# Moving 1 MB of output weights to the end of a decode kernel's load stream, laying W2 out anew, and turning the second MLP layer round

## The chip, the cores and the metric

The kernel runs on one core of a Trainium2 chip. The metric is the device time of one execution in microseconds (us); single executions of the kernel before spread over 1 to 1.5 us, so most experiments were timed in five rounds beside the kernel before on the same chip. The profile is one execution. Its time axis starts at the span's start, and all moments below ("at 664.7") are microseconds on that axis. The record calls an execution slow when it is over 1.5% above the fastest of its kernel.

## The reference, cut to what matters

```python
mod = silu(c) @ w_mod                      # six vectors per batch row: sa, ca, ga, sb, cb, gb
h = layernorm(x) * (1 + ca) + sa
x = x + ga * attention(h, k_cache, v_cache, wq, wo)   # 8 batch rows, 32 heads, 8 KV heads, 8192 cached keys
h = layernorm(x) * (1 + cb) + sb
r = relu(h @ w1 + b1)                      # 512 -> 1792
x = x + gb * ((r * r) @ w2 + b2)           # 1792 -> 512
```

Everything is bf16. The caches are 268 MB and are read once; the rest is small. The change aims at the last 30 us: the end of attention (`wo`), the first MLP layer (`w1`), the second (`w2`).

## The kernel before

One queue (SP's) loads nearly everything in order: modulation and query weights, then K and V tiles of 4 MB through a ring of four slots, and at the very end W1 and W2. The last V tile is loaded in four pieces. The 4096 x 512 output weights `wo` are loaded near the start, the last 1 MB of them separately.

```python
load(0); load(1)
...
d_woe = dma("sync", s_woe, ... A_wo[0:24 * DH, :] ...)            # 3 MB
d_wo = dma("sync", s_wo, lambda e: e.dma_start(                   # last 1 MB, packets of 1 KB
    wo_sb[:, 24:32, :], A_wo[24 * DH:, :].rearrange("(h dh) n -> dh h n", dh=DH)))
load(2); load(3)
...                                                               # at the last V tile:
d_w1 = dma("sync", s_w1, lambda e: e.dma_start(W1v, B_w1.rearrange("(k p) f -> p k f", p=128)), ...)
w2_r = B_w2.rearrange("(k p j) n -> p k j n", p=128, j=2)
d_w2 = [dma("sync", s_w2[i], lambda e, a=a, z=z: e.dma_start(W2v[:, a:z], w2_r[:, a:z]))
        for i, (a, z) in enumerate(((0, 4), (4, 7)))]             # 1 MB, then 0.75 MB
```

The MLP has the hidden units on partitions and the 8 batch rows as columns, in both layers. There are FT = 14 groups f of 128 hidden units. W2 comes in runs of two rows (2 KB), so a partition p of group f holds hidden unit 256*(f//2) + 2*p + f%2, and the first layer must read W1's columns with a step of 2 elements:

```python
for hh in range(2):
    for f in range(7 * hh, 7 * (hh + 1)):
        wcol = lambda k, f=f: W1v[:, k, 256 * (f // 2):256 * (f // 2 + 1)].rearrange(
            "p (q j) -> p j q", j=2)[:, f % 2, :]
        for k in range(KT):                                       # KT = 4
            t = op("tensor", lambda e: e.matmul(hT_ps[hh][:, f % 7, :], wcol(k), hbT[:, k, :], ...), [k_hb, d_w1])
    ... relu and square of the half, on VectorE ...
for f in range(FT):
    for k in range(KT):                                           # W2 is the stationary side, 8 columns stream
        t = op("tensor", lambda e: e.matmul(yT_ps[:, k, :], W2v[:, f // 2, f % 2, k * 128:(k + 1) * 128],
               hidT[:, f, :], ...), [k_sq[f // 7], d_w2[0 if f < 8 else 1]])
y2T = yT_ps * mod(5); yoT = y2T + x1T                             # 128 x 32, two VectorE operations
... four transposes, one copy on ACT, one on VectorE, two output DMAs of 4 KB
```

In a matmul call the stationary operand stands first (after the output), the streamed one second.

## Time and profile before

| | kernel before |
|---|---|
| median of 3 runs | 672.09 us (671.75 to 672.13) |
| span of the profiled execution | 669.4 us |
| share of the 16 DMA engines used by SP's queue | 99.0% |
| end of the chain | last W2 chunk lands, then about 2.1 us to the issue of the output |

The profile page's line of SP's DMA queue (packets, MB, share of 16 engines' span):

```profile
q1 hardware_dynamic: 13236, 283.65, 99.0%
```

The queue is full from start to end. Its stream decides the time; what counts beyond it is what must follow its last bytes. The end of the chain of waits, in order of time (start, duration, what):

```profile
642.46 1.41 SPq L552
643.92 21.47 DMA ring<-in_B_w_dram
665.43 0.82 PE PS L654 x24
```

The chain runs through the issue of the W2 DMAs, their landing, and the matmuls that waited for it. The timeline of the last microseconds (start, duration, engine, line, operation, output<-inputs, count, and in brackets how long the engine had idled and what ended that; PE is the matmul, PEld, further below, the load of a stationary operand):

```profile
661.91 1.68 PE L646 MATMUL PS<-hbT,ring 128*128 128x8 bf16 x56
...
663.61 0.99 PE L654 MATMUL PS<-hidT,ring 128*128 128x8 bf16 x32
...
665.43 0.81 PE L654 MATMUL PS<-hidT,ring 128*128 128x8 bf16 x24 [0.83 <-DMA ring<-in_B_w_dram]
666.28 0.19 DVE L658 TENSOR_TENSOR y2T<-PS,modT 128x32 f32<-128x32 f32 x1 [2.18 <-PE PS L654]
...
666.75 0.38 PE L665 MATMUL PS<-IDENT,yoT 128*8 128x128 bf16 x4 [0.51 <-DVE yoT L659]
667.16 0.37 ACT L672 ACTIVATE out_sb<-PS 8x256 bf16<-8x256 bf16 x1 [6.25 <-PE PS L665]
...
667.51 0.33 SPq L673 DMA_DIRECT2D out_dram<-out_sb  x1
```

L646 is the first layer: 56 matmuls in 1.68 us. L654 is the second: its first 32 matmuls run when the hidden values are there (663.6), its last 24 wait for the second W2 chunk until 665.43. Two small VectorE operations, transposes, copies, and the output is issued at 667.51.

The stages of the end (window, then its length and the busy time of PE, PEld, DVE, ACT and POOL with instruction counts, the granted TensorE clock with 1.00 as full speed, the share of the DMA engines in use, GB/s):

```profile
661.00:663.00 2.00, 2.00 (x50) 2.00 (x48) 0.66 (x4) 0.00 (x0) 0.00 (x0) 0.50 0.72 268
663.00:665.40 2.40, 1.59 (x55) 1.44 (x51) 0.76 (x4) 0.00 (x0) 0.00 (x0) 0.50 0.24 86
665.40:668.80 3.40, 1.19 (x28) 0.82 (x28) 0.66 (x3) 0.37 (x1) 0.00 (x0) 0.50 0.01 2
```

The clock is at half, and the DMA share falls to 0.72 and 0.24 while the stream still runs: the 16 engines don't finish together. The trace records 16 reports for each of these DMAs; those for the last W2 chunk come between 661.71 and 665.39. The waiting matmuls start after the last of them.

Two groups of 32 value matmuls of the same kernel, one at the low clock, one at the high one:

```profile
638.40 3.60 PE L525 MATMUL PS<-ring,Pm 128*32 128x512 bf16 x32 [0.54 <-DVE rinv L506]
...
642.98 1.91 PE L525 MATMUL PS<-ring,Pm 128*32 128x512 bf16 x32
```

They stream 512 columns each, in four column groups side by side: 3.60 us against 1.91.

### The profile page before, as it was taken

To read this page: it belongs to the slowest core of one execution; us is meant where nothing else is said; L and a number is where in the kernel's file an instruction comes from. 1 tells how busy PE (TensorE), PEld (TensorE's weight loads), DVE (VectorE), ACT (ScalarE), POOL (GpSimd) and SP (SyncE) were. 2 spreads that over 40 slices of the span, in tenths; PEclk is the share of its full clock that TensorE was granted. 3 is DMA by queue.
4 is the path that set the end of the run, shared out by engine and by line. 5 is a ranking of instruction groups with operands and counts; after the bars stand their busy time and mean duration, and the time that the engine had idled before them with its cause. 6 is when DMAs were issued, how large, how long until landed. Compare 5 with 4: busy or idle time off the path is not lost.

```text
span 669.4 us, 15944 instructions
## 1 busy us (share of the span) xinstructions
PE 480.1 (72%) x7372; PEld 344.2 (51%) x7372; DVE 299.3 (45%) x566; ACT 234.9 (35%) x280; POOL 16.7 (2%) x66
## 2 busy tenths in 40 slices
PE   2394963798639963699448987499736995389877
PEld 2383731675318741477316762287415773177545
DVE  2162731467316661367315672166513673146722
ACT  2061620366106640266204660056402662046610
POOL 7200000000000000000000000000000000000000
PEclk9996966799759986799867995599775997679986
DMA  9999999999999999999999999999999999999996
GB/s 375 433 402 436 419 434 432 433 427 435 431 435 431 425 433 437 433 429 431 433 435 433 423 435 431 437 427 429 433 437 435 423 431 433 437 433 425 431 416 245
DMA packets 13305, 283.95 MB, mean 424 GB/s; under 512 B 1218, under 2 KB 2275, under 8 KB 4708
## 3 DMA queue, kind: packets, MB, share of 16 engines
q1 hardware_dynamic: 13236, 283.65, 99.0%
q8 instruction: 13, 0.21, 0.1%
q14 instruction: 8, 0.07, 0.0%
q10 hardware_dynamic: 48, 0.02, 0.0%
HBM read 283.66 MB, written 0.01 MB: 424 GB/s over the span
## 4 chain that ended last, share of the span: by engine, by line
PE 55%; DMA 38%; DVE 3%; ACT 2%; issue 1%; SPq 0%
PE PS L427 36%; DMA ring<-in_A_k_cache_dram 35%; PE PS L442 9%; PE PS L486 4%; PE PS L525 4%; DMA ring<-in_B_w_dram 3%; ACT KTb L432 1%; ACT P_sb L477 1%; DVE m L447 1%; PE PS L505 1%; DVE Pm L499 0%; DVE rinv L506 0%; DVE rhs_r L503 0%; DVE Dm L470 0%; PE PS L472 0%
## 5 line engine op out<-in xcount | busy, mean ns | idle before, releaser
L432 ACT ACTIVATE KTb<-PS 128x1024 bf16<-128x1024 bf16 x192 | 196.5, 1024 | 372.4 <-PE PS L427 372.4
L427 PE MATMUL PS<-IDENT,ring 128*128 128x128 bf16 x4096 | 267.9, 228 | 51.6 <-DMA ring<-in_A_k_cache_dram 51.6
L427 PEld LDWEIGHTS PS<-IDENT,ring 128*128 128x128 bf16 x4096 | 247.3, 102 | 99.9 <-DMA ring<-in_A_k_cache_dram 52.7
L434 DVE COPY KTb<-PS 128x1024 bf16<-128x1024 bf16 x320 | 210.1, 687 | 152.0 <-PE PS L427 149.8
L525 PE MATMUL PS<-ring,Pm 128*32 128x512 bf16 x992 | 87.1, 513 | 58.5 <-DMA ring<-in_A_v_cache_dram 54.1
L534 DVE CAST O_sb<-PS 128x512 bf16<-128x512 f32 x31 | 21.4, 692 | 138.1 <-PE PS L525 138.1
L442 PE MATMUL PS<-KTb,Qb 128*32 128x512 bf16 x1024 | 78.8, 384 | 4.5 <-ACT KTb L432 4.5
L525 PEld LDWEIGHTS PS<-ring,Pm 128*32 128x32 bf16 x992 | 30.4, 120 | 96.3 <-DMA ring<-in_A_v_cache_dram 55.4
L486 PE MATMUL PS<-IDENT,P_sb 128*64 128x128 bf16 x512 | 26.2, 278 | 10.3 <-ACT P_sb L477 10.0
L538 PEld LDWEIGHTS PS<-SEL,O_sb 128*128 128x128 bf16 x124 | 5.3, 99 | 46.2 <-DVE O_sb L534 46.2
L486 PEld LDWEIGHTS PS<-IDENT,P_sb 128*64 128x64 bf16 x512 | 22.3, 147 | 13.0 <-ACT P_sb L477 13.0
L477 ACT ACTIVATE P_sb<-PS,negm 128x512 bf16<-128x512 f32 x32 | 21.5, 685 | 18.9 <-DVE negm L474 18.9
L499 DVE COPY Pm<-PS 64x512 bf16<-64x512 bf16 x48 | 20.2, 421 | 16.9 <-PE PS L486 15.9
L442 PEld LDWEIGHTS PS<-KTb,Qb 128*32 128x32 bf16 x1024 | 15.4, 94 | 21.1 <-ACT KTb L432 8.5
L538 PE MATMUL PS<-SEL,O_sb 128*128 128x8 bf16 x124 | 8.0, 170 | 24.9 <-DVE O_sb L534 24.9
L447 DVE TENSOR_REDUCE m<-PS 128x1 f32<-128x512 f32 x32 | 22.0, 689 | 6.6 <-PE PS L442 6.6
L496 ACT ACTIVATE Pm<-PS 64x512 bf16<-64x512 bf16 x16 | 9.5, 592 | 6.5 <-PE PS L486 6.4
L541 DVE TENSOR_TENSOR oTn<-PS,rinv 128x8 bf16<-128x8 f32 x31 | 6.0, 194 | 11.0 <-PE PS L538 11.0
L505 PE MATMUL PS<-rhs_r,ONES 128*128 128x32 f32 x16 | 4.6, 380 | 6.8 <-DVE rhs_r L503 6.8
L387 PE MATMUL PS<-haT,ring 128*128 128x8 bf16 x128 | 3.6, 168 | 7.5 <-DMA ring<-in_A_wq_dram 7.5
L472 PE MATMUL PS<-Dm,R 128*128 128x4 bf16 x8 | 1.4, 178 | 10.1 <-DVE Dm L470 10.1
L634 ACT ACTIVATE std<-PS,epst 128x8 f32<-128x8 f32 x1 | 0.3, 267 | 22.4 <-PE PS L632 22.4
(111 smaller groups left out, 97.1 us busy)
## 6 DMA issues: line engine op xcount, KB each, us to landing
ring<-in_A_k_cache_dram SPq DMA_DIRECT2D x32, 4096.0 KB, 34.1
ring<-in_A_v_cache_dram SPq DMA_DIRECT2D x31, 4096.0 KB, 28.1
ring<-in_A_wq_dram SPq DMA_DIRECT2D x1, 4096.0 KB, 20.3
ring<-in_w_mod_dram SPq DMA_DIRECT2D x1, 3072.0 KB, 10.4
wo_sb<-in_A_wo_dram SPq DMA_DIRECT2D x1, 3072.0 KB, 45.1
ring<-in_A_v_cache_dram SPq DMA_DIRECT2D x1, 2048.0 KB, 22.4
ring<-in_B_w_dram SPq DMA_DIRECT2D x1, 1792.0 KB, 18.9
wo_sb<-in_A_wo_dram SPq DMA_DIRECT2D x1, 1024.0 KB, 47.7
```

Source lines behind the costliest of these rows:

```text
L427: t = op("tensor", lambda e, j=j, i=i: e.matmul(STG[j][:, i, :], src[:, 32 * k + 8 * j + i, :], IDENT[:, :], is_transpose=True), [loaded[n ...
L432: stg_free[j] = op("scalar", lambda e, j=j, dst=dst: e.activation(dst, STG[j], ACT.Copy), [t], "scaP")
L434: stg_free[j] = op("vector", lambda e, j=j, dst=dst: e.tensor_copy(dst, STG[j]), [t], "vecP")
L442: t = op("tensor", lambda e, hf=hf, q=q, rhs=rhs: e.matmul(PS[32 * q:32 * (q + 1), k, :], Qb[:, 2 * p + hf, :], rhs, start=(p == 0 and hf ...
L447: return op("vector", lambda e: e.tensor_reduce(m4[:, k:k + 1], bank(k), AX.X, ALU.max), [t])
L477: exps.append(op("scalar", lambda e, k=k: e.activation(P_sb[:, k, :], bank(k), ACT.Exp, bias=negm[:, 0:1], scale=inv_sqrt, accum_out=rs4[: ...
L486: t = op("tensor", lambda e, k=k, i=i, hf=hf, src=src: e.matmul(STG[k][64 * hf:64 * (hf + 1), i, :], src, IDENT[:, :], is_transpose=True, ...
L499: done.append(op("vector", lambda e, dst=dst, frm=frm: e.tensor_copy(dst, frm), [t, k_pm], "vecP"))
L505: t = op("tensor", lambda e: e.matmul(tot_ps, ONES[:, :], rhs_r[:]), [t])
L525: t = op("tensor", lambda e, p=p, m=m, cg=cg, vt=vt, Obank=Obank: e.matmul(Obank[32 * cg:32 * (cg + 1), :], lhs[:, p, 32 * m:32 * m + 32], ...
L534: t = op("vector", lambda e, osb=osb, Obank=Obank: e.tensor_copy(osb, Obank), [t], "vecP")
L538: t = op("tensor", lambda e, i=i, osb=osb, oT_ps=oT_ps: e.matmul(oT_ps, osb[:, i * 128:(i + 1) * 128], SEL[:, i, :], start=(i == 0), stop= ...
```

## The change

Its intent: (1) the last values arrive earlier if the last 1 MB of `wo` comes behind them; (2) W2 in one run of 14 rows per partition needs fewer, larger DMA packets; (3) with the batch rows on partitions the second layer streams W2 instead of loading it, and its result needs no transposes; (4) a small last W2 chunk (2 of 14 groups) leaves little to do after the last landing.

```diff
-        d_wo = dma("sync", s_wo, ... last 1 MB of A_wo ...)        # was ahead of load(2)
...
+                    d_wo = dma("sync", s_wo, ... last 1 MB of A_wo ...)   # now ahead of d_w1
                     d_w1 = dma("sync", s_w1, ...)
-                    w2_r = B_w2.rearrange("(k p j) n -> p k j n", p=128, j=2)
+                    w2_r = B_w2.rearrange("(p f) n -> p f n", p=128)
...
-                            for i, (a, z) in enumerate(((0, 4), (4, 7)))]
+                            for i, (a, z) in enumerate(((0, F2), (F2, FT)))]      # F2 = FT - 2
...
-                wcol = lambda k, f=f: W1v[:, k, 256 * (f // 2):256 * (f // 2 + 1)].rearrange(
-                    "p (q j) -> p j q", j=2)[:, f % 2, :]
+                wcol = lambda k, f=f: W1v[:, k, :].rearrange("p (q f) -> p f q", f=FT)[:, f, :]
...
         for f in range(FT):
-            for k in range(KT):
-                    yT_ps[:, k, :], W2v[:, f // 2, f % 2, k * 128:(k + 1) * 128], hidT[:, f, :],
-                    [k_sq[f // 7], d_w2[0 if f < 8 else 1]])
-        ... y2T, yoT on 128 x 32, four transposes, two copies ...
+            for cc in range(2):
+                    yN_ps[64 * cc:64 * cc + B, :], hidT[:, f, :], W2v[:, f, 256 * cc:256 * (cc + 1)],
+                    ... tile_position=(0, 64 * cc) ..., [k_sq[f // 7], d_w2[0 if f < F2 else 1]])
+        t = y2N = yN_ps * gbN          # 72 x 256
+        t = out_sb = y2N + x1N         # 72 x 256
```

With it go: b1's 14 small loads at the same step as W1's columns; `gb` computed with batches on partitions at the start; the transposes of x, moved up between the layer norm's steps; 4 filler matmuls instead of 6 there (fillers multiply the identity by itself, nobody reads the result; they are there to keep PE busy).

Partition p now holds W2's rows 14*p to 14*p+13, so group f is the hidden units 14*p + f.

More of the change, by code (lines that the diff above doesn't have):

```diff
@@ L210, in bass_adaLN_cond__gqa_block_cached__dense_activation_squared_relu__decode_kernel @@
         xT = sb("xT", [128, KT, B], BF16)
-        modT = sb("modT", [128, 24, B], FP32)
+        modT = sb("modT", [128, 20, B], FP32)
+        gbN = sb("gbN", [128, 256], FP32)
         ca1 = sb("ca1", [128, KT, B], FP32)
@@ L227, in bass_adaLN_cond__gqa_block_cached__dense_activation_squared_relu__decode_kernel @@
         hbT = sb("hbT", [128, KT, B], BF16)
-        rT = sb("rT", [128, FT, B], FP32)
         hidT = sb("hidT", [128, FT, B], BF16)
-        y2T = sb("y2T", [128, KT, B], FP32)
-        yoT = sb("yoT", [128, KT, B], BF16)
         out_sb = sb("out_sb", [128, 256], BF16)
@@ L239, in bass_adaLN_cond__gqa_block_cached__dense_activation_squared_relu__decode_kernel @@
         hn = KF[0:B, 3072:4096].bitcast(FP32)
+        x1N = KF[:, 0:256]
+        y2N = KF[:, 512:1024].bitcast(FP32)
+        rT = KF[:, 1024:1024 + 2 * FT * B].bitcast(FP32).rearrange("p (f b) -> p f b", f=FT)
         slot = lambda i: RING[:, i, :]
@@ L283, in bass_adaLN_cond__gqa_block_cached__dense_activation_squared_relu__decode_kernel @@
         pool(lambda e: e.memset(ONES[:], 1.0))
+        k_gb0 = pool(lambda e: e.memset(gbN[:], 0.0))
         pool(lambda e: e.memset(ONESM[:], 1.0 / D))
@@ L320, in bass_adaLN_cond__gqa_block_cached__dense_activation_squared_relu__decode_kernel @@
         CH = (64, 96, 112, 128)
+        F2 = FT - 2
         def load(n):
@@ L370, in wm_cols @@
             return cols[:, 128 * (j % 4):128 * (j % 4 + 1)]
-        modT_ps = bank(0)[:, 0:24 * B].rearrange("p (j b) -> p j b", j=24)
-        for j in range(24):
+        gbN_ps = bank(1)[:, 0:256]
+        for cc in range(2):
+            for k in range(KT):
+                t = op("tensor", lambda e, cc=cc, k=k: e.matmul(
+                    gbN_ps[64 * cc:64 * cc + B, :], csT[:, k, :], wmod_v[:, k, 5 * D + 256 * cc:5 * D + 256 * (cc + 1)],
+                    start=(k == 0), stop=(k == KT - 1), tile_position=(0, 64 * cc)), [k_csT, d_wm])
+        k_gbN_ps = t
+        modT_ps = bank(0)[:, 0:20 * B].rearrange("p (j b) -> p j b", j=20)
+        for j in range(20):
             for k in range(KT):
@@ L396, in bass_adaLN_cond__gqa_block_cached__dense_activation_squared_relu__decode_kernel @@
         k_cb1 = op("vector", lambda e: e.tensor_scalar(cb1[:], mod(4), 1.0, None, ALU.add))
+        for cc in range(2):
+            rows = slice(64 * cc, 64 * cc + B)
+            k_gb = op("vector", lambda e, rows=rows: e.tensor_copy(gbN[rows, :], gbN_ps[rows, :]), [k_gbN_ps, k_gb0])
         stg_free = [None, None, None, k_QTm]
-        s_bank_free = [k_modT, None, None, None]
+        s_bank_free = [k_modT, k_gb, None, None]
         load(0)
@@ L407, in bass_adaLN_cond__gqa_block_cached__dense_activation_squared_relu__decode_kernel @@
             wo_e, A_wo[0:24 * DH, :].rearrange("(g p j) n -> p g (j n)", g=6, p=128)))
-        d_wo = dma("sync", s_wo, lambda e: e.dma_start(
-            wo_sb[:, 24:32, :], A_wo[24 * DH:, :].rearrange("(h dh) n -> dh h n", dh=DH)))
         load(2)
@@ L547, in bass_adaLN_cond__gqa_block_cached__dense_activation_squared_relu__decode_kernel @@
                     W1v = RING[:, s0, 0:KT * F].rearrange("p (k f) -> p k f", k=KT)
-                    W2v = RING[:, s0, KT * F:KT * F + FT * D].rearrange("p (k j n) -> p k j n", k=FT // 2, j=2)
+                    W2v = RING[:, s0, KT * F:KT * F + FT * D].rearrange("p (f n) -> p f n", f=FT)
+                    d_wo = dma("sync", s_wo, lambda e: e.dma_start(
+                        wo_sb[:, 24:32, :], A_wo[24 * DH:, :].rearrange("(h dh) n -> dh h n", dh=DH)))
                     d_w1 = dma("sync", s_w1, lambda e: e.dma_start(W1v, B_w1.rearrange("(k p) f -> p k f", p=128)),
                                [released[s0]])
-                    w2_r = B_w2.rearrange("(k p j) n -> p k j n", p=128, j=2)
+                    w2_r = B_w2.rearrange("(p f) n -> p f n", p=128)
                     d_w2 = [dma("sync", s_w2[i], lambda e, a=a, z=z: e.dma_start(W2v[:, a:z], w2_r[:, a:z]))
-                            for i, (a, z) in enumerate(((0, 4), (4, 7)))]
+                            for i, (a, z) in enumerate(((0, F2), (F2, FT)))]
                     attn_ps = bank(4)[:, 0:KT * B].rearrange("p (k b) -> p k b", k=KT)
                     hT_ps = [bank(i)[:, 0:7 * B].rearrange("p (f b) -> p f b", f=7) for i in range(2)]
-                    yT_ps = bank(2)[:, 0:KT * B].rearrange("p (k b) -> p k b", k=KT)
-                    b1v = b1_row[:].rearrange("o (k p j) -> o k j p", p=128, j=2)
+                    yN_ps = bank(2)[:, 0:256]
+                    b1v = b1_row[:].rearrange("o (p f) -> o f p", f=FT)
                     pP = bank(6)[:, 0:192].rearrange("p (j g b) -> p j g b", j=4, g=6)
@@ L570, in bass_adaLN_cond__gqa_block_cached__dense_activation_squared_relu__decode_kernel @@
                         op("tensor", lambda e, f=f: e.matmul(
-                            hT_ps[f // 7][:, f % 7, :], b1v[:, f // 2, f % 2, :], ONE8[:, :],
+                            hT_ps[f // 7][:, f % 7, :], b1v[:, f, :], ONE8[:, :],
                             start=(f % 7 == 0), stop=False, skip_group_check=True), [d_b2, s_bank_free[f // 7]])
-                    for k in range(KT):
-                        op("tensor", lambda e, k=k: e.matmul(
-                            yT_ps[:, k, :], b2_row[:, k * 128:(k + 1) * 128], ONE8[:, :],
-                            start=(k == 0), stop=False, skip_group_check=True), [s_bank_free[2]])
+                    for cc in range(2):
+                        op("tensor", lambda e, cc=cc: e.matmul(
+                            yN_ps[64 * cc:64 * cc + B, :], ONE8[:, :], b2_row[:, 256 * cc:256 * (cc + 1)],
+                            start=True, stop=False, tile_position=(0, 64 * cc), skip_group_check=True),
+                            [s_bank_free[2]])
                     for g in range(6):
@@ L624, in bass_adaLN_cond__gqa_block_cached__dense_activation_squared_relu__decode_kernel @@
                                                     stop=(k == KT - 1)), [k_x1])
-        pe_fill(6, 7)
+        x1N_ps = bankb(4)[:, 0:256]
+        for cc in range(2):
+            for k in range(2):
+                k_x1N = op("tensor", lambda e, k=k, cc=cc: e.matmul(
+                    x1N_ps[64 * cc:64 * cc + B, 128 * k:128 * (k + 1)], x1T[:, 2 * cc + k, :], IDENT[:, :],
+                    is_transpose=True, tile_position=(0, 64 * cc)), [k_x1])
+        pe_fill(4, 7)
         bc = lambda ap: ap.unsqueeze(1).to_broadcast([128, KT, B])
@@ L651, in bass_adaLN_cond__gqa_block_cached__dense_activation_squared_relu__decode_kernel @@
                 hidT[:, fs, :], rT[:, fs, :], rT[:, fs, :], ALU.mult), [t]))
+        for cc in range(2):
+            rows = slice(64 * cc, 64 * cc + B)
+            k_x1c = op("scalar", lambda e, rows=rows: e.activation(x1N[rows, :], x1N_ps[rows, :], ACT.Copy), [k_x1N])
         for f in range(FT):
-            for k in range(KT):
-                t = op("tensor", lambda e, f=f, k=k: e.matmul(
-                    yT_ps[:, k, :], W2v[:, f // 2, f % 2, k * 128:(k + 1) * 128], hidT[:, f, :],
-                    start=False, stop=(f == FT - 1), skip_group_check=True),
-                    [k_sq[f // 7], d_w2[0 if f < 8 else 1]])
-        t = op("vector", lambda e: e.tensor_tensor(y2T[:], yT_ps, mod(5), ALU.mult), [t])
-        t = op("vector", lambda e: e.tensor_tensor(yoT[:], y2T[:], x1T[:], ALU.add), [t])
-        o_ps = bankb(3)[:, 0:256]
+            for cc in range(2):
+                t = op("tensor", lambda e, f=f, cc=cc: e.matmul(
+                    yN_ps[64 * cc:64 * cc + B, :], hidT[:, f, :], W2v[:, f, 256 * cc:256 * (cc + 1)],
+                    start=False, stop=(f == FT - 1), tile_position=(0, 64 * cc), skip_group_check=True),
+                    [k_sq[f // 7], d_w2[0 if f < F2 else 1]])
+        NR = 64 + B
+        t = op("vector", lambda e: e.tensor_tensor(y2N[0:NR, :], yN_ps[0:NR, :], gbN[0:NR, :], ALU.mult), [t])
+        t = op("vector", lambda e: e.tensor_tensor(out_sb[0:NR, :], y2N[0:NR, :], x1N[0:NR, :], ALU.add), [t, k_x1c])
         outf = out.rearrange("b s d -> (b s) d")
@@ L663, in bass_adaLN_cond__gqa_block_cached__dense_activation_squared_relu__decode_kernel @@
         for cc in (1, 0):
-            for k in range(2):
-                tt = op("tensor", lambda e, k=k, cc=cc: e.matmul(
-                    o_ps[64 * cc:64 * cc + B, 128 * k:128 * (k + 1)], yoT[:, 2 * cc + k, :], IDENT[:, :],
-                    is_transpose=True, tile_position=(0, 64 * cc)), [t])
             rows = slice(64 * cc, 64 * cc + B)
-            if cc == 0:
-                tt = op("vector", lambda e, rows=rows: e.tensor_copy(out_sb[rows, :], o_ps[rows, :]), [tt])
-            else:
-                tt = op("scalar", lambda e, rows=rows: e.activation(out_sb[rows, :], o_ps[rows, :], ACT.Copy), [tt])
             d_o.append(dma(("sync", "scalar")[cc], s_out[cc], lambda e, cc=cc, rows=rows: e.dma_start(
-                outf[:, 256 * cc:256 * (cc + 1)], out_sb[rows, :]), [tt]))
+                outf[:, 256 * cc:256 * (cc + 1)], out_sb[rows, :]), [t]))
         Pg.wait("sync", d_o)
```

## The prediction

> **What bounds the kernel now.** The span is 669.4 us in the profile. The DMA queue view gives the 16 DMA engines a 99% share, the windows view about 430 GB/s from start to end; counting packets in flight I find no gap except the first 2.1 us and the tail. The chain of waits ends: last half of the second-layer weights W2 lands (DMA, 21.5 us, wait ends 665.43), 24 matmuls (0.81 us), two small vector operations, four transposes, evictions (0.37 and 0.28 us), output DMAs issued at 667.51 and 667.57. So only two things count: when the stream's last bytes land, and what follows them (2.1 us to the issue).
>
> The landings in the trace are staggered: the 16 engines report the last W2 chunk from 661.71 to 665.39, and the DMA share is 0.72 and 0.24 in the last two windows. A DMA's semaphore is full only when all its engines have reported (the Trainium skill, "DMA: Bandwidth & Descriptors", why a DMA increments its semaphore by 16); the trace agrees, the matmuls waited for the 665.39 one. The slowest engine sets everything.
>
> **The stream.** Total bytes stay. Moving 1 MB of output weights (64 packets of 1 KB per engine, about 2.65 us of an engine, from packets of 41 to 48 ns) from the start to behind the last values lets the last values land near 653.8 instead of 656.4; the output weights land near 656.4, W1 at 661.0 as before. It moves no end. W2 in one run per partition: packets of 12 KB and 2 KB instead of 56 of 2 KB per engine. From measured packets (2 KB 86 ns, overlapped 79; 32 KB 1218 ns) I estimate 4.3 us instead of 4.4: 0.1 us gained. First chunk (12 of 14) lands near 664.65, last near 665.3.
>
> **Compute before W2.** Attention output, layer norm and first layer move up by about 1 us, then the first layer meets W1's landing: hidden values ready near 663.3 (were 664.1). Off the chain: W2 lands later.
>
> **After the landing.** Old: 24 weight-load-bound matmuls of 8 columns. New: 24 matmuls of 256 columns become possible only at 664.7, when the large chunk lands, then 4 more. The granted clock is 0.50 from 661 on (windows view), and PE idles before W2 lands, so I expect it stays. The skill ("TensorE: Matmul & The Clock Gate", back-to-back issue gap) gives N/1.2 ns cold; the trace agrees: 32 value matmuls of 512 columns in four column groups took 3.60 us cold, 1.91 warm. Two column groups side by side: 14 x 256/1.2 = 2.99 us plus 0.25 drain, so the sum is complete near 667.95 (old 666.25). Multiply and add on 256 columns: about 0.42 us each (128x32 took 0.19, 128x512 0.69). Issue near 668.9 instead of 667.5. Removing transposes and evictions (about 0.75 us) doesn't pay for it. The small last chunk gains nothing: it lands while the first is still being multiplied.
>
> **Predicted: 673.2 us**, range 671.7 to 674.1. Chances: faster by over 2% 0.005, within 2% 0.99, slower 0.005.
>
> **Right if** the new second layer's matmuls start at a wait for the large W2 chunk near 664.7, take about 3 us at clock 0.5, start last ones without a wait, the stream still ends near 665.3, and output is issued near 668.9.
>
> **Wrong if** the clock is 1.0 there (then 1.5 us, and the total is about 0.2 us under the old); if the large descriptors or the reordering narrow the stagger of engines; if the two column groups don't overlap (3 us more).

## The result, and the profile after

Four runs took 672.62 us (672.47 to 673.0), four of the kernel before beside them 671.92 us (671.55 to 672.13). The ratio is 1.0012, 95% interval [0.9994, 1.0029]. A ratio is the mean time of one kernel's fast runs over that of the other's of the same rounds, so not quite the ratio of the medians. The difference, 0.7 us by medians, is not clear of noise by this interval. The two profiled executions differ by 1.4 us of span (669.4 and 670.8); the one of before, at 671.45 us, was one of its fastest.

```profile
q1 hardware_dynamic: 12596, 283.65, 98.8%
```

The queue sends 640 packets less (12,596), and its stream ends where it did: the trace has the last W2 report at 665.18, before it was 665.39. The end of the chain of waits after:

```profile
660.00 1.51 PE PS L430 x14
661.51 3.30 PE PS L665 x56
664.81 3.10 PE PS L676 x28
```

There is no DMA in it. Before, the last steps were a landing and 24 matmuls; now they are fillers, first layer (L665), second layer (L676), all PE. The timeline:

```profile
661.30 3.51 PE L665 MATMUL PS<-hbT,ring 128*128 128x8 bf16 x56
...
664.74 3.15 PE L676 MATMUL PS<-ring,hidT 128*8 128x256 bf16 x28
664.85 0.22 DVE L668 TENSOR_SCALAR KTb<-PS 128x56 f32<-128x56 f32 x1 [1.22 <-PE PS L665]
...
667.94 0.42 DVE L681 TENSOR_TENSOR KTb<-PS,gbN 72x256 f32<-72x256 f32 x1 [2.62 <-PE PS L676]
668.39 0.42 DVE L682 TENSOR_TENSOR out_sb<-KTb 72x256 bf16<-72x256 f32 x1
668.84 0.32 SPq L687 DMA_DIRECT2D out_dram<-out_sb  x1
```

Two things are to be seen. The second layer takes 3.15 us and ends the sum at 667.9, so the output is issued at 668.84 instead of 667.51. And the first layer takes 3.51 us instead of 1.68, with the same count of the same shapes. Its last matmul ends about where the second layer begins: L676 has no bracket, it waited for no DMA.

```profile
661.00:663.00 2.00, 2.00 (x34) 2.00 (x33) 0.00 (x0) 0.00 (x0) 0.00 (x0) 0.50 0.55 221
663.00:665.40 2.40, 2.40 (x39) 2.14 (x39) 0.87 (x4) 0.00 (x0) 0.00 (x0) 0.50 0.15 58
665.40:668.80 3.40, 2.49 (x24) 1.27 (x20) 0.83 (x2) 0.00 (x0) 0.00 (x0) 0.50 0.02 5
```

PE is busy through both windows up to 665.4, at clock 0.50, where before it idled for 0.8 us waiting for W2. The large W2 chunk's last report is at 664.55, just before the first layer ends. So two limits came within 0.2 us of each other, and this trace alone can't say what removing one of them is worth.

### The profile page after: what moved, and what is told of

The parts are those of the page before. It is cut to its first block, busy times and chain, and to the rows that moved or that the text cites. A ratio compares the mean times of both kernels' runs of the same rounds, so it can differ in the third digit from the quotient of the medians.

```text
span 670.8 us, 15868 instructions
## 1 busy us (share of the span) xinstructions
PE 483.1 (72%) x7332; PEld 345.3 (51%) x7332; DVE 300.2 (45%) x567; ACT 235.1 (35%) x281; POOL 17.1 (3%) x67
## 3 DMA queue, kind: packets, MB, share of 16 engines
q1 hardware_dynamic: 12596, 283.65, 98.8%
## 4 chain that ended last, share of the span: by engine, by line
PE 55%; DMA 38%; DVE 3%; ACT 2%; issue 1%; ACTq 0%
PE PS L438 35%; DMA ring<-in_A_k_cache_dram 33%; PE PS L453 9%; DMA ring<-in_A_v_cache_dram 4%; PE PS L536 3%; PE PS L497 3%; ACT KTb L443 1%; DMA KTb<-in_A_x_dram 1%; ACT P_sb L488 1%; DVE m L458 1%; PE PS L516 1%; PE PS L665 0%; PE PS L676 0%; DVE Pm L510 0%; PE PS L610 0%
```

## The experiments

Three theories of what holds up the second layer:

- Theory L: the landing of the large W2 chunk (12 of 14 groups).
- Theory S: the first layer, slowed by the step of 14.
- Theory T: both, tied; then removing one alone gives almost nothing.

The numbers together (PE time of the first layer, start of the second, issue of the output, all from the profiled execution; the timed runs in rounds of five are against kernels before of 671.88, 671.97 and 672.15 us):

| run | median us | ratio to before, 95% | first layer | second starts | issue |
|---|---|---|---|---|---|
| changed kernel | 672.62 | 1.0012 [0.9994, 1.0029] | 3.51 | 664.74 | 668.84 |
| e1 step 2 | 672.77 | 1.0012 [0.9999, 1.0026] | 1.68 | 665.01 | 669.10 |
| e2 three chunks | 672.16 | 1.0004 [0.9990, 1.0017] | 3.51 | 664.93 | 669.03 |
| e3 both | 671.33 | 0.9992 [0.9978, 1.0006] | 1.64 | 662.84 | 667.48 |
| e4 four groups | 671.98 | 1.0001 [0.9988, 1.0015] | 3.50 | 664.97 | 667.33 |
| e5 step 2, five chunks | 671.02 | 0.9985 [0.9972, 0.9999] | 1.63 | 663.35 | 667.21 |
| e6 before + layout | 672.95 | 1.0023 [1.0010, 1.0037] | 3.52 | 666.03 | 668.93 |
| e7 before + `wo` late | 671.64 | 0.9993 [0.9979, 1.0007] | 1.63 | 663.81 | 667.71 |
| e8 changed, `wo` early | 675.20 | 1.0049 [1.0035, 1.0063] | 3.51 | 666.18 | 670.18 |
| e12 before + `wo` late, four chunks | 671.09 | 0.9985 [0.9971, 0.9999] | 1.64 | 662.95 | 667.08 |

All kernels of this section gave correct results.

### e1: the step back to 2

```diff
-                    w2_r = B_w2.rearrange("(p f) n -> p f n", p=128)
+                    w2_r = B_w2.rearrange("(k p j) n -> p k j n", p=128, j=2)
...                                                               # b1's columns likewise
-                wcol = lambda k, f=f: W1v[:, k, :].rearrange("p (q f) -> p f q", f=FT)[:, f, :]
+                wcol = lambda k, f=f: W1v[:, k, 256 * (f // 2):256 * (f // 2 + 1)].rearrange(
+                    "p (q j) -> p j q", j=2)[:, f % 2, :]
```

> The changed kernel, but W2 laid out in runs of two rows as before, so the first layer reads W1's columns at a step of 2 elements instead of 14; second layer, chunks (12 and 2 of 14) and everything else stay. Theory L (the landing of the large W2 chunk gates the second layer): its matmuls start at a DMA wait near 664.6 us, total within 0.2 us of the changed kernel. Theory S (the first layer, slowed from 1.7 to 3.5 us by the wide step, gates it alone): they start near 663.3 and the total falls by about 1.4 us. Theory T (two limits that happen to tie, 664.55 and 664.74): the first layer falls to about 1.7 us, yet the total falls by only 0.1 to 0.2 us. All three need the first layer at about 1.7 us; if it stays at 3.5 us, the step is not what slows it.

Timeline of e1, first and second layer:

```profile
661.37 1.68 PE L667 MATMUL PS<-hbT,ring 128*128 128x8 bf16 x56
...
665.01 3.15 PE L678 MATMUL PS<-ring,hidT 128*8 128x256 bf16 x28 [1.96 <-DMA ring<-in_B_w_dram]
```

The first layer is back at 1.68 us, and the total did not fall (672.77 us, where theory T allowed 0.1 to 0.2 us less than 672.62; in this execution the large chunk landed 0.3 us later than in the changed kernel's). Now the second layer has a bracket: it idled 1.96 us for W2's large chunk, whose last report came at 664.87 here. Theory S is out; this was the wait that the prediction named.

### e2: three chunks, the step stays

```diff
-                            for i, (a, z) in enumerate(((0, F2), (F2, FT)))]
+                            for i, (a, z) in enumerate(((0, 6), (6, 12), (12, 14)))]
```

> The changed kernel, W2 in three chunks of 6, 6 and 2 instead of 12 and 2; the step of 14 stays. Theory L: the second layer starts near 663.3 us, total falls by about 1.3 us. Theories S and T: it still starts after the first layer's last matmul near 664.75, total within 0.2 us of the changed kernel.

```profile
661.50 3.51 PE L665 MATMUL PS<-hbT,ring 128*128 128x8 bf16 x56
...
664.93 3.15 PE L676 MATMUL PS<-ring,hidT 128*8 128x256 bf16 x28
```

The first chunk of 6 groups had landed by 663.01, yet the second layer began at 664.93, straight after the first. Theory L alone is out. The total was 672.16 us, 0.46 us under the changed kernel's median from other rounds: more than the 0.2 us expected. The two intervals overlap widely and the profiled output was issued no earlier (669.03), so I don't read it as a gain. But the profiled execution was the slowest of the five (672.86 us), and the other four took 672.05 to 672.21 without a trace: a gain of some tenths is not excluded.

### e3: both

> Both edits: step of 2 and chunks of 6, 6 and 2. Theory T: only both together help; the second layer starts near 663.0 us, takes about 3.1 us at clock 0.5, output is issued near 667.2, and the total falls by about 1.5 us against the changed kernel, to just under the kernel before. Theory L expects no more than the split alone gives, theory S no more than the step alone.

```profile
660.95 1.64 PE L667 MATMUL PS<-hbT,ring 128*128 128x8 bf16 x56
...
662.84 1.45 PE L678 MATMUL PS<-ring,hidT 128*8 128x256 bf16 x12 [0.25 <-DVE KTb L670]
...
664.66 1.87 PE L678 MATMUL PS<-ring,hidT 128*8 128x256 bf16 x16 [0.38 <-DMA ring<-in_B_w_dram]
...
667.48 0.32 SPq L689 DMA_DIRECT2D out_dram<-out_sb  x1
```

Each alone moved the issue of the output by +0.2 to +0.3 us; both together moved it by -1.36 us, and the total to 671.33 us, 1.3 us under the changed kernel (1.5 were expected). That is theory T: two limits in parallel, tied. The second layer now starts at 662.84, runs its first 12 matmuls, and waits until 664.66 for the middle chunk.

### e4: four column groups instead of two

```diff
-            for cc in range(2):
-                    yN_ps[64 * cc:64 * cc + B, :], hidT[:, f, :], W2v[:, f, 256 * cc:256 * (cc + 1)],
+            for cc in range(4):
+                    yN_ps[32 * cc:32 * cc + B, :], hidT[:, f, :], W2v[:, f, 128 * cc:128 * (cc + 1)],
...
-        for cc in (1, 0):              # two output DMAs, rows of 512 bytes
+        for cc in (1, 0, 3, 2):        # four output DMAs, rows of 256 bytes
```

> The changed kernel, the second layer's 512 outputs on four column groups of 128 instead of two of 256 (56 matmuls), the two vector operations on 128 columns, four output DMAs of 2 KB. If columns streamed per group at the cold clock set the layer's time, it falls from 3.15 us to about 1.6 to 1.8 us [...], the vector operations from 0.42 to about 0.28 us each, and the total by about 1.5 us, after 0.3 us lost to two more DMA issues. If the matmuls are bound by issue instead, 56 of them take no less than 28 did and only 0.3 us is gained, taken back by the issues.

```profile
664.97 1.66 PE L675 MATMUL PS<-ring,hidT 128*8 128x128 bf16 x56
...
666.68 0.29 DVE L680 TENSOR_TENSOR KTb<-PS,gbN 104x128 f32<-104x128 f32 x1 [1.33 <-PE PS L675]
...
667.33 1.01 SPq L686 DMA_DIRECT2D out_dram<-out_sb  x2
```

The layer behaved as expected: 56 matmuls of 128 columns in 1.66 us, half of 3.15, at the same clock. VectorE took 0.29 us for each operation. The output was issued 1.5 us earlier, but the total fell by only 0.6 us. The loss is at the output: from the first issue at 667.33 to the span's end at 670.56 are 3.2 us, against 1.9 us (668.84 to 670.76) in the changed kernel. I had allowed 0.3 us for this, it was 1.3. SP issued its second DMA only at 668.03, so 0.7 us of the loss is the wait for that issue; the last reports of the writes came at 670.09. What the other 0.6 us come from, the number of DMAs or their rows of 256 bytes, no run separates.

### e5: step of 2, five chunks

```diff
+                            for i, (a, z) in enumerate(((0, 6), (6, 8), (8, 10), (10, 12), (12, 14)))]
```

> The changed kernel with the step of 2 (as in the run with both edits) and W2 in five chunks of 6, 2, 2, 2 and 2. In the run with both edits the second layer still waited at 664.66 us for its middle chunk and then needed 1.87 us for 16 matmuls, while the last chunk came about 0.6 us later. If the wait for chunk granularity is what is left, the matmuls keep step with the stream (0.63 us for a chunk, 0.43 us for its 4 matmuls), end about 0.65 us behind the last landing near 665.2, output is issued near 666.7 and the total falls by 0.7 us against that run, to about 670.6, 1.2 us under the kernel before. If more, smaller DMAs cost stream time, the last landing moves past 665.5 and eats it.

```profile
663.35 2.91 PE L678 MATMUL PS<-ring,hidT 128*8 128x256 bf16 x28 [0.19 <-DMA ring<-in_B_w_dram]
...
665.82 0.15 PEld L678 LDWEIGHTS PS<-ring,hidT 128*8 128x8 bf16 x4 [0.25 <-DMA ring<-in_B_w_dram]
666.31 0.42 DVE L683 TENSOR_TENSOR KTb<-PS,gbN 72x256 f32<-72x256 f32 x1 [2.64 <-PE PS L678]
```

The second layer runs in step with the stream, waits 0.4 us for DMAs in all, loads its last operands at 665.82 when the last chunk is in, and the sum is ready 0.49 us later. 671.02 us is 0.95 us under the kernel before and 1.6 us under the changed one. The expectation was 670.6, with the last landing near 665.2; had small DMAs cost stream time, it would move past 665.5. It came at 665.78. But in this execution the stream was late before the first W2 chunk (W1's last report at 661.39 instead of 660.91), and from there to W2's last report it took 4.39 us, no more than e3 with three chunks (4.44). So the smaller chunks are not the cause. One piece of luck belongs to this profile: the granted clock rose to 1.0 at 665.89, just as the last chunk's matmuls ran; whether it did so in the other four executions is not known.

### e6: the kernel before with the new layout alone

> The kernel before with nothing but the new layout: W2 in one run of 14 rows per partition (chunks 8 and 6), so W1's and b1's columns are read at a step of 14. If the step is what slows weight loads, whatever follows: the first layer takes about 3.5 us instead of 1.68, ends near 665.4 when the last chunk has landed, the 56 old matmuls follow at 30 ns each, and the total rises by 0.8 to 1.4 us. If the slow first layer belongs to something else of the change (transposes before it, the copies on ACT), it stays at 1.7 us and the total stays.

```profile
662.65 3.52 PE L645 MATMUL PS<-hbT,ring 128*128 128x8 bf16 x56
...
666.03 1.64 PE L653 MATMUL PS<-hidT,ring 128*128 128x8 bf16 x56
```

The old kernel, given nothing but the layout, has a first layer of 3.52 us too. So the step is the cause, not the transposes or copies that the change put nearby. Its 14 small loads of b1 took 1.00 us of PE instead of 0.50. The total rose by 0.98 us by medians, within the expected 0.8 to 1.4. Two of its five runs took 674.2 and 674.6 us; no trace was taken of those.

### e7: the kernel before with the move alone

> The kernel before with only the last 1 MB of output weights moved behind the last values. The stream's bytes are the same, so its last landing stays near 665.4, the old second layer waits for it, and the total stays within 0.3 us; only attention's end and the first layer's start come about 0.7 us earlier, the first layer meeting W1's landing near 661.0.

```profile
661.36 1.63 PE L646 MATMUL PS<-hbT,ring 128*128 128x8 bf16 x56
...
663.81 1.05 PE L654 MATMUL PS<-hidT,ring 128*128 128x8 bf16 x32 [0.82 <-DMA ring<-in_B_w_dram]
...
665.64 0.80 PE L654 MATMUL PS<-hidT,ring 128*128 128x8 bf16 x24 [0.78 <-DMA ring<-in_B_w_dram]
```

Attention waited for the output weights (they landed at 656.64), the first layer started 0.55 us earlier than before, and the last 24 matmuls waited for W2's last chunk all the same, until 665.64. The total was 671.64 us; the interval includes 1. The move alone is worth nothing that these runs can tell.

### e8: the changed kernel with the move undone

> The changed kernel with the 1 MB of output weights back at the start. The stream's end stays near 665.2, but attention ends about 0.6 us later, and since the slow first layer (3.5 us) now runs into the second, the total rises by about 0.6 us against the changed kernel. If the landing of the large chunk alone set the second layer's start, the total would stay within 0.2 us.

```profile
662.74 3.51 PE L665 MATMUL PS<-hbT,ring 128*128 128x8 bf16 x56
...
666.18 3.04 PE L676 MATMUL PS<-ring,hidT 128*8 128x256 bf16 x28
```

Here I was wrong in size: 675.20 us, 2.6 us over the changed kernel instead of 0.6. The profiled execution (673.86 us, the fastest of the five) explains half of it. The first layer starts 1.4 us later than in the changed kernel. That delay is there from the start of the tail: with the values arriving late, PE begins the last steps of attention at 649.79 instead of 648.30, and since it is busy without a break for the next 6.6 us in both, nothing of it is won back. (b1's slow loads, 1.00 us instead of 0.50, lengthen this stretch against the kernel before, but they are in both kernels compared here.) With the first layer slow, the second starts 1.44 us later and the output is issued 1.34 us later. The other executions were up to 2 us slower still, without a trace. What they lost remains open; e6, the other kernel with `wo` early and the step of 14, has two such executions too. So the early arrival of the values mattered in the changed kernel. That it did so because the slow first layer had made the compute chain critical fits this profile, where the second layer again waits for no DMA, and e7, where the move gained nothing; no run undoes the move with the step at 2.

### e9 and e10: the step itself

The layout with runs of 7 rows, and with runs of one row.

```diff
+                    w2_r = B_w2.rearrange("(k p j) n -> p k j n", p=128, j=7)     # e9; e10: j=1
```

> The changed kernel with W2 in runs of 7 rows, so W1's columns are read at a step of 7 elements (14 bytes); chunks of 7, 5 and 2. A look at the first layer's 56 weight loads alone. If the cost grows with the bytes a load spans, a step of 7 takes about half way, 45 ns each (2.5 us in all); if it is a threshold between 7 and 14 elements, 30 ns each (1.7 us); if odd steps or steps that miss 4 bytes are bad, 63 ns or more.

> The changed kernel with W2 in runs of one row (1 KB packets), so W1's columns are read contiguously; chunks of 6, 6 and 2. If the 30 ns for a load at a step of 2 is already a floor of the array, the first layer still takes about 1.7 us; if packing matters, it takes less. The stream ends about 0.15 us later from smaller packets.

Line views of the first layer's weight loads (duration of one in ns, minimum, median and maximum; start of the first and the last), e9 and then e10:

```profile
L666 PEld LDWEIGHTS PS<-hbT,ring x56: 137/152/156, 661.0 to 664.0; 128*128 128x128 bf16 x56
```

```profile
L667 PEld LDWEIGHTS PS<-hbT,ring x56: 104/104/108, 661.0 to 662.4; 128*128 128x128 bf16 x56
```

From first to last start, divided by 55, a load takes 54 ns at a step of 7 and 27 ns at a step of 1. At a step of 2 it was 27 ns (e3) to 29 ns (e1, before), at 14 it was 61 ns (changed kernel). The start-up phase of both kernels has 32 loads at a step of 4, which took 33 ns each, and contiguous ones beside them that took 27 ns. The first layers ran at clock 0.50; for the start-up phase the trace has no clock record. The clock seems to matter little, though: b1's 14 loads of one row each ran at clock 1.0 and took 58 ns at a step of 14 (changed kernel, 648.5) against 25 ns at a step of 2 (before, 650.0). So steps of 1 and 2 cost the same, and from there the cost climbs with the step, steeply between 4 and 7 and little after that. These are times from start to start; a single load lasts longer (the 104 and 152 ns of the views), because loads overlap. None of my three shapes for e9 was right: it was not half way (45 ns), not the floor (30), not more than at 14 (63). Whether an odd step has a part in it is open.

### e11: the same second layer at the full clock

```diff
+        pe_fill(70, 7)                 # between the first layer and the second
```

> The changed kernel with 70 filler matmuls of 128 columns put between the first layer and the second, only to raise the granted clock; the total gets worse by about 5 us and that is not the question. If the clock sets the second layer's 3.15 us, the same 28 matmuls take about 1.7 us once the clock is 1.0 [...]. If something else (two weight loads of 8 columns per row, issue) sets it, they stay above 2.5 us.

```profile
664.63 6.79 PE L430 MATMUL PS<-IDENT 128*128 128x128 bf16 x70
...
671.35 1.70 PE L677 MATMUL PS<-ring,hidT 128*8 128x256 bf16 x28
```

The fillers raised the clock to 1.0 at 670.4, and the 28 matmuls took 1.70 us. The clock sets the layer's time. The fillers themselves cost over 5 us here (677.68 us).

### e12: the old second layer with better ordered loads

```diff
-                            for i, (a, z) in enumerate(((0, 4), (4, 7)))]
+                            for i, (a, z) in enumerate(((0, 3), (3, 5), (5, 6), (6, 7)))]
```

together with the move of `wo`.

> The kernel before in its old second layer, with the move of the output weights and W2 in chunks of 6, 4, 2 and 2 rows of 128: what the order of loads alone can give without turning the second layer round. Last landing near 665.4, then only 8 matmuls (0.4 us), the two vector operations, transposes and evictions (1.25 us): output issued near 667.0 instead of 667.5, total about 0.5 us under the kernel before and about 0.3 us over the run with five chunks.

```profile
665.43 0.38 PE L654 MATMUL PS<-hidT,ring 128*128 128x8 bf16 x8 [0.26 <-DMA ring<-in_B_w_dram]
665.84 0.19 DVE L658 TENSOR_TENSOR y2T<-PS,modT 128x32 f32<-128x32 f32 x1 [2.64 <-PE PS L654]
...
667.08 0.32 SPq L673 DMA_DIRECT2D out_dram<-out_sb  x1
```

671.09 us, 1.06 us under the kernel before and not to be told from e5; the intervals of both end just short of 1. After the last landing only 8 matmuls remain (0.38 us), and the transposes and copies that the change removed are still there. So turning the second layer round gained nothing beyond this that the runs can tell; small last chunks did, once nothing else held the layer up. The move of `wo` alone left the total within noise (e7); small chunks without the move were not run.

## Why the prediction was right or wrong

The predicted total was 673.2 us, range 671.7 to 674.1; it was 672.62. Point by point:

- **What bounds the kernel: right.** The stream's end hardly moved (665.39 to 665.18, predicted 665.3). The last values landed at 653.47 (predicted 653.8), the output weights at 656.35 (656.4), W1 at 660.91 (661.0), the large W2 chunk at 664.55 (664.65). The small gain from larger packets is there as well (4.3 us instead of 4.4 were predicted): from W1's last report to W2's last took 4.25 to 4.31 us in the six runs with one run of 14 rows per partition, and 4.37 to 4.47 us in the six with runs of two rows. e7 agrees that the move by itself gains nothing in the old kernel that the runs can tell.
- **The second layer: right.** It started at 664.74 (predicted 664.7), took 3.15 us at clock 0.50 (predicted 2.99 plus 0.25), VectorE took 0.42 us twice, as estimated, and the output was issued at 668.84 (predicted 668.9). e11 (1.70 us at the full clock) and e4 (1.66 us at half the columns per group) show that streamed columns at the granted clock set it. But the reason given for the clock was wrong: PE was to idle before W2 lands. PE's records are busy all of the time from 661 to 665.4, and the clock stayed at 0.50 all the same. That was luck.
- **"Hidden values ready near 663.3": wrong.** They were ready at 665.3, because the first layer took 3.51 us; another 0.3 us is its start at 661.30, behind filler matmuls, and not at W1's landing. I had carried over its 1.68 us, although the diff changes the step at which it reads W1. The term of the sum that was mis-sized is the weight load: 61 ns at a step of 14 instead of 29 ns at 2. e6 shows the step as the cause, e9 and e10 how it grows.
- **"Start at a wait for the large W2 chunk": wrong in the trace; that the moment came out right was luck.** The first layer, not the landing, released the second. The landing came 0.2 us earlier, and in e1 the layer began 0.14 us after it, so the two ends nearly tied. Had W2 been chunked finely, the slow first layer, which my sum left out, would have cost 1.5 us at the issue of the output and 0.8 us of the total (e2 against e3).
- **"The small last chunk gains nothing": right** for this chunking. e5 and e12 show what it takes: no slow first layer, and chunks fine enough that the layer keeps step with the stream.
- **The size of the total: a bit high.** The issue of the output moved by 1.33 us, as predicted (1.4). The medians differ by 0.7 us. The profile that the prediction started from was of a fast execution, 0.47 us under the later median of the kernel before.

## What to carry to other kernels

When a change alters how a tensor lies in memory, cost every reader of it again, not only the DMA: here 640 fewer packets bought some 0.15 us of the stream, and the step of 14 that came with them doubled the first layer. When two limits end within a fraction of a microsecond of each other, taking away either one looks useless; try both together before giving up on either (e1, e2, e3). At the end of a DMA-bound stream, order the loads and cut the last ones so that compute keeps step with it; that gave the 1 us, with either form of the layer (e5, e12).

## What the Trainium skill lacked or had wrong

- "TensorE: Matmul & The Clock Gate", LDWEIGHTS (loading the stationary operand): it gives the load as columns / 1.2 ns, 107 ns for 128 columns. One load lasted 104 ns here, which agrees, but loads overlap: contiguous ones of 128 bf16 columns started every 27 ns. Its section on weight-path perf modes names a fast load and calls its read pattern "packed or strided", with no cost for the step. A note on cachelines in "SBUF — State Buffer" (Door 1: The DMA port swizzle) calls steps of up to 8 bf16 elements free, which doesn't hold for these loads: the runs show 27 ns at steps 1 and 2, 33 at 4, 54 at 7 and 61 at 14 elements.
- The same page, Part 1: the clock rises after a busy window of about 3.4 us. On what counts as busy it says only, in Part 4, that transposes don't count the same way. In the changed kernel PE's records are busy 84% of the time from 656 to 661 and all of it from 661 to 665.4 (from 661.3 to 664.7 with matmuls of 8 columns), and the clock stayed at 0.50; 70 back-to-back fillers of 128 columns, from 664.6 on, raised it at 670.4 (e11).
- "DMA: Bandwidth & Descriptors": its sections say that the engines of one DMA finish independently, which the runs confirm, but not how far apart they get. For W1 and W2, after 640 us of the stream, the first and the last report of one transfer lay 3.3 to 4.3 us apart over all runs; for the 4 MB that landed at 21 to 22 us it was 1.0 to 2.4 us. The windows show what it costs: DMA shares of 0.72 (before) and 0.55 (after) from 661 to 663.
- The same page gives rows of 512 bytes as the least for line rate. Two output DMAs with such rows took 1.9 us from issue to the span's end, four with rows of 256 bytes 3.2 us, 0.7 us of it the later second issue (e4). No run here separates the rows' size from the number of DMAs in the rest.
